# Retention, then a truncated-quadratic MoE layer, then a SoLU layer: blocks of 512 tokens, weight conversion kept off GpSimd, activation as a maximum read from PSUM, decay tables in the attention, state decay on ScalarE

## The chip, the cores and the metric

The kernel runs on one core of one Trainium2 chip. A core has TensorE (PE in the profile, its weight loads PEld), VectorE (DVE), ScalarE (ACT), GpSimd (POOL) and SyncE (SP), which here issues every DMA. The metric is the device time of one execution in microseconds; a version is judged by the median of its runs.

## The reference

Three layers follow each other, all in float32.

```python
# attention: B, H, S, D = 4, 8, 768, 64; gamma = 1 - 2**(-5 - head)
for t in range(S):
    state = gamma * state + k[t] (outer) v[t]
    y[t] = q[t] @ state / sqrt(D)
x = y as [3072 tokens, 512]
# first layer: 512 -> 2048 -> 512
h = x @ w_in
g = h where h >= 1, 0 where h <= -1, else (h + 1)**2 / 4
x2 = g @ w_out
# second layer: 512 -> 1024 -> 512
u = h2 * softmax(h2), h2 = x2 @ w2_in
out = (layer norm of u, times g_ln) @ w2_out
```

The weights arrive as float64.

## The kernel before

**Phase A** is attention and the first layer. The 3072 tokens go in blocks of BLK = 384 (eight blocks), and d_ff = 2048 in 16 parts f of 128. A *slot* is one block with one part f. `moe_h` (line 319) makes h of the slot with 12 matmuls (L325): each float32 operand is held as a sum of two float32r parts, and the three products high-high, low-high, high-low are added in PSUM over four parts of d_model. The activation follows (L337 to L342), its result is again split in two (L121 on ScalarE, L122 on VectorE), and `moe_out` (line 347), two slots later, adds 12 more matmuls (L360) into four PSUM banks `acc`. At the end of a block the four banks are copied out (L368 to L373) and stored to DRAM. 128 slots in all. Their order is not block by block at first: block 0 with f 0 to 5, block 1 with f 0 to 11, block 0 with f 6 to 15, block 1 with f 12 to 15, then whole blocks (L275). So new weights are taken up slowly; an unfinished block's sum is parked in DRAM (`x2p`).

**Weights** are loaded by L130 and converted by `conv_w` (L133): ScalarE takes the high word's absolute value (L139) and the low word (L142), VectorE clips, shifts and merges the sign (L140, L143, L144), GpSimd adds the two as integers (L145), ScalarE rounds to the high part (L149), and the low part is a subtraction (L150), on GpSimd for 34 of the 48 conversions and on VectorE for 14. Phase A needs 32 conversions, one pair per part f; the 16 conversions of the second layer run in the last block (L417 to L419), two per slot, those of w2_out with one more VectorE step (L147).

**Attention** goes in 24 units of 128 tokens with all heads, `attention` (L157), each a generator whose steps are taken in given slots (L283 to L290). The first six units (NF32) work in plain float32, the others split queries and keys in float32r parts (L197 to L200, L206 to L210). A unit scales v by a decay column (L183), masks the scores (L211 or L215), multiplies scores by v (L233) and the state by the queries (L229), scales the result by a table (L238), splits it (L121, L122), and renews the state (L245 to L254).

**Phase B** is the second layer, 24 tiles of 128 tokens, lines 432 to 537: 24 matmuls L464, softmax and norm on VectorE and ScalarE, 8 transposes L505, 24 matmuls L516.

**Order.** Every engine runs its own list in order. The lists are made by a scheduler that takes the order of issue in the program as priority; attention units from the seventh on and the loads of the first eight parts f are raised by 1000. PSUM has four banks `acc` (shared with the attention of block 0 and phase B), two banks for h (`ps_h`) and two for attention (`ps_a`).

Of the kernel before, what the change touches and what calls it, by code (L numbers as in the profile page):

```python
# [26 lines left out]
BLK = 384  # L27
# [6 lines left out]
# words of the high half of a float64, read as float32: 2^-127 and the largest float32r  # L34
LO_I = (0,1)
LO_O = range(4,16)
LO_2 = 0
V_POOL = 3
DMA_ORDER = -99
PSV = 0  # L40
HPW = 0
HPL = 8
SA = 6
SB = 12
LD = 6
CL = 3
HPC = 0
PHB = 3
XL_POOL = 0
QL_POOL = 0  # L50
NF32 = 6
WM_BUFS = 3
WP_BUFS = 3
QK_BUFS = 3
QS_BUFS = 1
KV_BUFS = 1
QN_BUFS = 1
GATE = 6
SM_BUFS = 3
# [14 lines left out]
def kernel(  # L74
# [23 lines left out]
    wp = ctx.enter_context(tc.tile_pool(name="wp", bufs=33))  # L98
# [8 lines left out]
    neg1 = const.tile([128, 1], F32, tag="neg1", name="neg1")  # L107
    mask = const.tile([128, 1, C], F32, tag="mask", name="mask")
# [8 lines left out]
    def split(src, hi, lo, hi_eng=None, lo_eng=None):  # L117
        if hi_eng is ve:
            ve.tensor_copy(hi, src)
        else:  # L120
            sc.activation(hi, src, AF.Copy)  # L121
        (lo_eng or ve).tensor_tensor(out=lo, in0=src, in1=fl(hi), op=ALU.subtract)  # L122

# [9 lines left out]
    def conv_w(raw, scale=None, lo_eng=None):  # L133
        lw, hw = raw[:, :, 0], raw[:, :, 1]
        m = cv.tile([128, 512], F32, tag="wm", name="wm", bufs=WM_BUFS)
        p = cv.tile([128, 512], F32, tag="wp", name="wp", bufs=WP_BUFS)
# [14 lines left out]
        return w[:, 0, :], w[:, 1, :]  # L151

# [1 line left out]
    # Heads go in pairs (even, odd); the even one takes partitions 0-63 of queries, keys and  # L154
    # state, the odd one 64-127, and TensorE works on both halves of its array at a time.
    # In x the halves of pairs 2 and 3 are swapped, and so are the rows of w_in.
    def attention(u, env):  # L157
# [26 lines left out]
        sm = []  # L184
        if exact:
            yield
            qp = [ppool.tile([128, NPAIR, C], F32, tag=ptag, name=f"qp{o}") for o in range(2)]
            for p in range(NPAIR):
                for o in range(2):
                    r = slice(64 * o, 64 * o + 64)  # L190
                    pe.matmul(qp[o][:, p, :], qk[r, 1, p, :], qk[r, 0, p, :], start=True, stop=True)
        for o in range(2):
            if not exact:
                raw = qks[o]
                kh = cv.tile([128, NPAIR, C], F32R, tag="wm", name="kh", bufs=WM_BUFS)
                qs = attp.tile([128, NPAIR, 2, C], F32R, tag="qs", name="qs", bufs=QS_BUFS)
# [186 lines left out]
    for s in range(min(min(sched), -LD - 1), 0):  # L383
# [5 lines left out]
        if s == DMA_ORDER:  # L389
            order.close()  # L390
# [207 lines left out]
```

## Time and profile before

| what | value |
|---|---|
| median of 3 runs | 972.96 us (972.27 to 973.82) |
| profiled execution, its span | 969.7 us |
| TensorE busy | 936.3 us, 97% |
| weight loads busy | 856.5 us, 88% |
| VectorE busy | 741.9 us, 77% |
| ScalarE busy | 455.6 us, 47% |
| GpSimd busy | 201.0 us, 21% |
| instructions | 14961 |

The profile is of one execution. It gives the span from the first to the last instruction; the time of an execution also has what lies around the span, and the median is 3.3 us above it. Times of single matmuls overlap, since the next one enters the array before the last has left: the distance between starts is what one costs.

### The profile page before, as it was taken

Reading aid. Unit: us, or ns where it says so; the run is one execution under the profiler, and the core shown is the slowest. Engines: PE = TensorE matmul, PEld = TensorE weight load, DVE = VectorE, ACT = ScalarE, POOL = GpSimd, SP = SyncE. Lnnn points to the kernel's source line nnn. Section 1 sums busy time; section 2 is a strip of 40 time slices with the busy share of each in tenths; the row PEclk is TensorE's granted clock in tenths of the full one; section 3 lists DMA queues with packets and bytes.
Section 4 is the critical chain, followed back from the end, with each engine's and each line's share of the span. In section 5 each row is a group of like instructions: output and inputs, shape, how many; then the busy total and the mean of one; then the engine's idle time right before and its main releaser. Section 6 shows DMA issues by size and latency. Waiting matters only on the chain.

```text
span 969.7 us, 14961 instructions
## 1 busy us (share of the span) xinstructions
PE 936.3 (97%) x5560; PEld 856.5 (88%) x5560; DVE 741.9 (77%) x1593; ACT 455.6 (47%) x905; POOL 201.0 (21%) x177
## 2 busy tenths in 40 slices
PE   8798898999999999999999999989999999999998
PEld 7588888999999999999999999969888888888886
DVE  6999999877666666655664574997788888888885
ACT  3557676545545545544553464664433333333322
POOL 2754544212211221111220120662000000000000
PEclk9899999999999999999999999999999999999999
DMA  9902823154233232420320230311111011010000
GB/s 366 360 1 82 250 82 114 48 169 126 79 98 116 92 97 80 128 77 22 114 72 12 107 143 1 122 64 69 66 55 42 35 55 54 23 61 28 22 23 33
DMA packets 31465, 87.03 MB, mean 90 GB/s; under 512 B 4384, under 2 KB 10656, under 8 KB 31392
## 3 DMA queue, kind: packets, MB, share of 16 engines
q1 hardware_dynamic: 31392, 86.08, 26.9%
q8 instruction: 44, 0.72, 0.3%
q14 instruction: 29, 0.24, 0.1%
HBM read 71.90 MB, written 14.16 MB: 89 GB/s over the span
## 4 chain that ended last, share of the span: by engine, by line
PE 74%; DVE 18%; issue 3%; ACT 2%; DMA 2%; SPq 0%; POOL 0%; ACTq 0%; DVEq 0%; POOLq 0%
PE acc L360 19%; PE hp L325 19%; PE h2p L464 14%; PE op L516 14%; DVE wm L144 3%; DVE cs L340 3%; DVE wm L140 2%; PE pv L233 2%; PE tp L505 2%; DVE gl L122 2%; PE qp L206 2%; DVE wm L143 2%; DVE cs L337 2%; PE pv L229 2%; DVE w L150 1%
## 5 line engine op out<-in xcount | busy, mean ns | idle before, releaser
L360 PE MATMUL acc<-gh,w 128*128 128x384 f32 x1024 | 214.3, 339 | 9.6 <-ACT gh L121 7.6
L325 PE MATMUL hp<-xh,w 128*128 128x384 f32 x1024 | 209.6, 340 | 5.6 <-ACT rr L338 3.9
L360 PEld LDWEIGHTS acc<-gh,w 128*128 128x128 f32 x1024 | 180.1, 189 | 15.4 <-ACT gh L121 10.4
L325 PEld LDWEIGHTS hp<-xh,w 128*128 128x128 f32 x1024 | 179.0, 189 | 12.2 <-ACT rr L338 6.2
L338 ACT ACTIVATE rr<-hp,neg 128x384 f32<-128x384 f32 x128 | 74.1, 579 | 161.4 <-DVE cs L337 161.2
L340 DVE TENSOR_TENSOR cs<-cs,rr 128x384 f32<-128x384 f32 x128 | 86.0, 672 | 77.7 <-ACT cs L339 76.8
L360 PE MATMUL acc<-gl,w 128*128 128x384 f32 x512 | 121.7, 338 | 4.8 <-DVE gl L122 4.8
L325 PE MATMUL hp<-xl,w 128*128 128x384 f32 x512 | 111.8, 338 | 0.0
L122 DVE TENSOR_TENSOR gl<-cs,gh 128x384 fp32r<-128x384 f32 x128 | 85.5, 668 | 26.7 <-ACT gh L121 24.5
L121 ACT ACTIVATE gh<-cs 128x384 fp32r<-128x384 f32 x128 | 66.8, 522 | 65.7 <-DVE cs L340 65.5
L464 PE MATMUL h2p<-w,x2h 128*128 128x512 f32 x384 | 97.4, 395 | 0.0
L360 PEld LDWEIGHTS acc<-gl,w 128*128 128x128 f32 x512 | 90.3, 188 | 8.1 <-DVE gl L122 7.5
L337 DVE TENSOR_SCALAR cs<-hp 128x384 f32<-128x384 f32 x128 | 70.5, 551 | 32.3 <-PE hp L325 31.8
L325 PEld LDWEIGHTS hp<-xl,w 128*128 128x128 f32 x512 | 91.7, 190 | 0.5 <-DVE xl L122 0.3
L516 PE MATMUL op<-w,lh 128*128 128x512 f32 x384 | 91.4, 390 | 0.2 <-ACT lh L121 0.2
L145 POOL TENSOR_TENSOR wm<-wm,wp 128x512 int32<-128x512 int32 x48 | 69.1, 1440 | 88.0 <-DVE wm L144 70.6
L516 PEld LDWEIGHTS op<-w,lh 128*128 128x128 f32 x384 | 71.9, 188 | 15.4 <-ACT lh L121 0.5
L464 PEld LDWEIGHTS h2p<-w,x2h 128*128 128x128 f32 x384 | 70.5, 188 | 13.5
L339 ACT ACTIVATE cs<-cs,half 128x384 f32<-128x384 f32 x128 | 77.6, 606 | 2.5 <-DVE cs L337 2.5
L150 POOL TENSOR_TENSOR w<-wm,w 128x512 fp32r<-128x512 f32 x34 | 49.6, 1461 | 52.2 <-ACT w L149 51.9
L211 POOL TENSOR_SCALAR_AFFINE_SELECT sm<-sm 128x512 f32<-128x512 f32 x36 | 36.3, 1010 | 99.6 <-DVE sm L210 99.6
L254 POOL TENSOR_TENSOR state<-state,gdec 64x256 f32<-64x256 f32 x32 | 22.0, 688 | 165.1 <-DVE state L253 163.9
(79 smaller groups left out, 1299.7 us busy)
## 6 DMA issues: line engine op xcount, KB each, us to landing
qk<-in_qk_t_dram SPq DMA_DIRECT2D x72, 256.0 KB, 3.8
kv<-in_kv_t_dram SPq DMA_DIRECT2D x24, 512.0 KB, 3.8
w_raw<-in_w_in_dram SPq DMA_DIRECT2D x24, 512.0 KB, 7.3
w_raw<-in_w_out_dram SPq DMA_DIRECT2D x24, 512.0 KB, 6.7
x2d<-xs SPq DMA_DIRECT2D x32, 192.0 KB, 2.0
x2r<-x2d SPq DMA_DIRECT2D x8, 768.0 KB, 4.3
out_dram<-o SPq DMA_DIRECT2D x24, 256.0 KB, 2.0
qn<-in_qk_t_dram SPq DMA_DIRECT2D x15, 256.0 KB, 3.1
```

What stands on the lines that cost most here:

```text
L121: sc.activation(hi, src, AF.Copy)
L122: (lo_eng or ve).tensor_tensor(out=lo, in0=src, in1=fl(hi), op=ALU.subtract)
L145: gp.tensor_tensor(out=mi, in0=mi, in1=p.bitcast(I32), op=ALU.add)
L150: (lo_eng or gp).tensor_tensor(out=w[:, 1, :], in0=m, in1=fl(w[:, 0, :]), op=ALU.subtract)
L325: pe.matmul(hp, l[:, k * 128:(k + 1) * 128], r[:, k, :], start=(n == 0), stop=(n == 3 * KD - 1))
L337: ve.tensor_scalar(cs, hp, -1.0, 1.0, op0=ALU.max, op1=ALU.min)
L338: sc.activation(rr, hp, AF.Relu, bias=neg1)
L339: sc.activation(cs, cs, AF.Square, bias=half, scale=0.5)
L340: ve.tensor_tensor(out=cs, in0=cs, in1=rr, op=ALU.add)
L360: pe.matmul(acc[d][:, :BLK], l[:, d * 128:(d + 1) * 128], r, start=(first and m == 1), stop=(last and m == 3))
L464: pe.matmul(hps[n], l[:, k, :], w2i[k, n][part], start=(m == 0), stop=(m == 3 * KD - 1))
L516: pe.matmul(op, l[:, f, :], w2o[f][part], start=(n == 0), stop=(n == 3 * NF2 - 1))
```

## The change

- BLK is 512: six blocks, 96 slots, each with 24 matmuls of 512 columns in place of 384. NF32 becomes 8 (two blocks of four units). The attention's places in the slots follow the new block (PER = 4), and weights are converted four slots ahead instead of three, loaded seven ahead instead of six.
- `conv_w` has no GpSimd step: the integer add and the low part go to VectorE; the scale of w2_out goes into the rounding on ScalarE and into the low part's instruction. The second layer's conversions go at 2, 1, 2, 1, ... per slot from f = 2 to 12.
- The activation is max(h, ((clip(h) + 1)/2)^2): ScalarE's relu (L338) is gone, and VectorE's last step reads h from PSUM.
- The mask and both decays of the scores become one table `dmat` by which VectorE multiplies the scores; the scaling of v, the scaling of the result (L238) and the masking on GpSimd (L211) go. Instead the queries for the state are multiplied by `qdec` (VectorE for the first eight units, GpSimd after), and the keys for the state by the decay column on GpSimd, except in the last unit of a sequence. `tables` makes the two tables at the start.
- The state is decayed by four ScalarE instructions before the sum, not on GpSimd after it. The state's matmuls are issued before the result is split.
- Fewer buffers: sm and qk have 2 instead of 3; xs shares three buffers with cs. The raised priority of the first weight loads goes.

```diff
-BLK = 384
+BLK = 512
...
-LD = 6
-CL = 3
+LD, CL = 7, 4
+NF32 = 2 * CPB
+GATE = 2 * CPB
+PER = 4
...
-        gp.tensor_tensor(out=mi, in0=mi, in1=p.bitcast(I32), op=ALU.add)
-        if scale is not None:
-            ve.tensor_scalar(m, m, scale, None, op0=ALU.mult)
+        ve.tensor_tensor(out=mi, in0=mi, in1=p.bitcast(I32), op=ALU.add)
         w = wp.tile([128, 2, 512], F32R, tag="w", name="w")
-        sc.activation(w[:, 0, :], m, AF.Copy)
-        (lo_eng or gp).tensor_tensor(out=w[:, 1, :], in0=m, in1=fl(w[:, 0, :]), op=ALU.subtract)
+        hi, lo = w[:, 0, :], w[:, 1, :]
+        if scale is None:
+            sc.activation(hi, m, AF.Copy)
+            ve.tensor_tensor(out=lo, in0=m, in1=fl(hi), op=ALU.subtract)
+        else:
+            sc.activation(hi, m, AF.Copy, scale=scale)
+            ve.scalar_tensor_tensor(lo, m, scale, fl(hi), op0=ALU.mult, op1=ALU.subtract)
...
-        (gp if u >= V_POOL else ve).tensor_tensor(out=kv[:, 1], in0=kv[:, 1], in1=vdec.to_broadcast([128, H, D]), op=ALU.mult)
...
+            if not first:
+                qn = attp.tile([128, NPAIR, C], F32, tag="qn", name="qn", bufs=1)
+                ve.tensor_tensor(out=qn, in0=qk[:, 0], in1=qdec, op=ALU.mult)
+        elif not first:
+            gp.tensor_tensor(out=qn, in0=qn, in1=qdec, op=ALU.mult)
+        if not last:
+            gp.tensor_tensor(out=kv[:, 0], in0=kv[:, 0], in1=vdec.to_broadcast([128, H, D]), op=ALU.mult)
...
-                gp.affine_select(out=t, in_=t, pattern=[[0, NPAIR], [1, C]], compare_op=ALU.is_ge,
-                                 fill=0.0, base=0, channel_multiplier=-1)
+                ve.tensor_tensor(out=t, in0=t, in1=dmat[:, o], op=ALU.mult)
...
-        for g in range(2):
-            d = slice(2 * g, 2 * g + 2)
-            ve.tensor_tensor(out=xt[:, d], in0=pv[g], in1=xtab[:, d], op=ALU.mult)
-        split(xt, xh[:, :, tk], xl[:, :, tk], lo_eng=gp if XL_POOL else None)
+        split(pv, xh[:, :, tk], xl[:, :, tk])
...
+        if not first:
+            for p in range(NPAIR):
+                sc.activation(st[:, p, :], st[:, p, :], AF.Copy, scale=gdec[:, p, :])
...
-                ve.tensor_tensor(out=d, in0=sp[r], in1=d, op=ALU.add)
-                gp.tensor_tensor(out=d, in0=d, in1=g, op=ALU.mult)
+                ve.tensor_tensor(out=st[r, :, r], in0=sp[r], in1=st[r, :, r], op=ALU.add)
...
+    def tables():
+        nc.sync.dma_start(vdec, vdec_d)
+        for o in range(2):
+            for dup in range(2):
+                nc.sync.dma_start(dmat[64 * dup:64 * dup + 64, o], xtab_d[64 * o:64 * o + 64])
+        nc.sync.dma_start(gdec, gdec_d)
+        nc.sync.dma_start(qdec, xtab_d)
+        for o in range(2):
+            ve.tensor_tensor(out=dmat[:, o], in0=dmat[:, o], in1=vdec[:, o::2].to_broadcast([128, NPAIR, C]), op=ALU.mult)
+            gp.affine_select(out=dmat[:, o], in_=dmat[:, o], pattern=[[0, NPAIR], [1, C]], compare_op=ALU.is_ge,
+                             fill=0.0, base=0, channel_multiplier=-1)
+        gp.tensor_tensor(out=qdec, in0=qdec, in1=gdec.to_broadcast([128, NPAIR, C]), op=ALU.mult)
...
-        x = (k - 3, SA - 3 + k, X2 + 3 * k)[blk] if blk < 3 else base[blk] - NF + PER * k + SHIFT
+        x = (k - CPB, SA - CPB + k)[blk] if blk < 2 else base[blk] - NF + PER * k + 2
...
-            sc.activation(rr, hp, AF.Relu, bias=neg1)
-            sc.activation(cs, cs, AF.Square, bias=half, scale=0.5)
-        ve.tensor_tensor(out=cs, in0=cs, in1=rr, op=ALU.add)
+        sc.activation(cs, cs, AF.Square, bias=half, scale=0.5)
+        ve.tensor_tensor(out=cs, in0=hp, in1=cs, op=ALU.max)
...
-            if f >= 2:
-                w2_conv(2)
-                w2_step(2)
+            if 2 <= f < 13:
+                w2_conv(2 - f % 2)
+                w2_step(2 - f % 2)
```

## Rows read from the trace of the kernel before

**Rows 1.** Stretches: length; busy us of PE, PEld, DVE, ACT, POOL; clock; DMA share; GB/s.
```profile
5.60:71.30 65.70, 56.28 (x433) 47.02 (x432) 62.82 (x95) 31.54 (x55) 37.70 (x31) 0.92 0.63 250
71.30:155.00 83.70, 73.48 (x413) 68.32 (x414) 80.01 (x122) 59.48 (x113) 36.85 (x27) 0.98 0.42 131
...
200.00:600.00 400.00, 399.50 (x2650) 388.12 (x2649) 254.58 (x466) 197.41 (x402) 70.99 (x74) 1.00 0.30 92
600.00:686.00 86.00, 79.36 (x430) 73.89 (x430) 70.04 (x100) 49.81 (x92) 39.22 (x27) 1.00 0.21 73
686.00:969.70 283.70, 279.72 (x1329) 233.00 (x1327) 234.38 (x742) 88.99 (x191) 0.00 (x0) 1.00 0.12 42
```

**Rows 2.** Chain of waits that ended last, by line, of the first 160 us alone.
```profile
by line: issue 11.7%; DVE wm L144 10.2%; DVE wm L140 9.3%; DVE cs L340 8.4%; DVE wm L143 7.6%; DVE gl L122 7.0%; DVE cs L337 5.5%; DVE w L150 5.2%; DMA kv<-in_kv_t_dram 3.5%; DVE xl L122 2.7%; PE acc L360 2.2%; DVE sm L215 2.2%; DMA w_raw<-
```

**Rows 3.** Timeline of PE: start us, length us, line, shape, count.
```profile
401.86 1.55 PE L360 MATMUL acc<-gh,w 128*128 128x384 f32 x8
403.24 0.85 PE L360 MATMUL acc<-gl,w 128*128 128x384 f32 x4
...
404.28 0.64 PE L206 MATMUL qp<-qs,kh 128*128 128x256 f32 x4
404.76 1.21 PE L325 MATMUL hp<-xh,w 128*128 128x384 f32 x6
...
818.02 3.79 PE L516 MATMUL op<-w,lh 128*128 128x512 f32 x16
821.64 1.98 PE L516 MATMUL op<-w,ll 128*128 128x512 f32 x8
```

**Rows 4.** Lines of PE from 200 to 600 us, by form: count, busy us, mean ns.
```profile
L360 PE MATMUL acc<-gh,w 128*128 128x384 f32 x654 | 134.7, 335 | 0.5 <-DVE xs L373 0.5
...
L325 PE MATMUL hp<-xl,w 128*128 128x384 f32 x324 | 69.9, 334 | 0.0
...
L233 PE MATMUL pv<-sm,kv 128*64 128x128 f32 x256 | 20.5, 280 | 0.0
```

**Rows 5.** Lines of VectorE and GpSimd, first 155 us, by form: count, busy us, mean ns.
```profile
L144 DVE SCALAR_TENSOR_TENSOR wm<-w_raw,wm 128x512 uint32<-128x512 uint32 x28 | 24.3, 869 | 0.1
...
L150 DVE TENSOR_TENSOR w<-wm,w 128x512 fp32r<-128x512 f32 x11 | 12.7, 1151 | 0.0
...
L145 POOL TENSOR_TENSOR wm<-wm,wp 128x512 int32<-128x512 int32 x28 | 39.4, 1409 | 51.3 <-DVE wm L144 37.1 <-ACT cs L339 8.3 <-ACT wp L142 2.0
```

**Rows 6.** Single lines over the whole span: count, min/median/max ns, first and last start.
```profile
L140 DVE TENSOR_SCALAR wm<-wm x48: 410/420/1522, 15.4 to 657.1; 128x512 f32<-128x512 f32 x48
...
L144 DVE SCALAR_TENSOR_TENSOR wm<-w_raw,wm x48: 672/681/1776, 17.4 to 659.8; 128x512 uint32<-128x512 uint32 x48
...
L337 DVE TENSOR_SCALAR cs<-hp x128: 542/550/560, 31.2 to 678.5; 128x384 f32<-128x384 f32 x128
...
L340 DVE TENSOR_TENSOR cs<-cs,rr x128: 544/558/1651, 36.5 to 680.3; 128x384 f32<-128x384 f32 x128
...
L183 POOL TENSOR_TENSOR kv<-kv,vdec x21: 1042/1045/1494, 24.4 to 537.8; 128x512 f32<-128x512 f32 x21
```

**Rows 7.** Timeline around 103 us: VectorE, then GpSimd.
```profile
103.56 0.42 DVE L143 TENSOR_SCALAR wm<-wm 128x512 uint32<-128x512 uint32 x1
103.89 1.78 DVE L150 TENSOR_TENSOR w<-wm,w 128x512 fp32r<-128x512 f32 x1
105.59 0.54 DVE L337 TENSOR_SCALAR cs<-hp 128x384 f32<-128x384 f32 x1
106.06 0.68 DVE L144 SCALAR_TENSOR_TENSOR wm<-w_raw,wm 128x512 uint32<-128x512 uint32 x1
106.66 0.41 DVE L140 TENSOR_SCALAR wm<-wm 128x512 f32<-128x512 f32 x1
...
103.72 1.40 POOL L145 TENSOR_TENSOR wm<-wm,wp 128x512 int32<-128x512 int32 x1 [2.70 <-DVE wm L144]
```

**Rows 8.** The page's costliest groups: one line of ScalarE, count, busy us, mean ns.
```profile
L338 ACT ACTIVATE rr<-hp,neg 128x384 f32<-128x384 f32 x128 | 74.1, 579 | 161.4 <-DVE cs L337 161.2
```

More of the change, by code (lines that the diff above doesn't have):

```diff
@@ L115, in fl, with split @@
         return t.bitcast(F32)
[L117 to L122, printed above, removed]
+    def split(src, hi, lo):
+        sc.activation(hi, src, AF.Copy)
+        ve.tensor_tensor(out=lo, in0=src, in1=fl(hi), op=ALU.subtract)
     wi, wo = {}, {}
@@ L163, in attention @@
         exact = u < NF32
-        kv = (wp if exact else attp).tile([128, 2, H, D], F32, tag="w" if exact else "kv", name="kv", bufs=None if exact else KV_BUFS)
+        kv = (wp if exact else attp).tile([128, 2, H, D], F32, tag="w" if exact else "kv", name="kv",
+                                          bufs=None if exact else 1)
+        qn = None
         with (ExitStack() if u < GATE else tc.issue_after(state["last_w"].ins)):
@@ L224, in attention @@
         tk = slice(cb * C, cb * C + C)
-        pv = [ppool.tile([128, 2, C], F32, tag=ptag, name=f"pv{g}") for g in range(2)]
+        pv = ppool.tile([128, NPAIR, C], F32, tag=ptag, name="pv")
         if not first:
             for p in range(NPAIR):
-                pe.matmul(pv[p // 2][:, p % 2, :], st[:, p, :], qn[:, p, :],
-                          start=(p % 2 == 0), stop=False, skip_group_check=True)
+                pe.matmul(pv[:, p, :], st[:, p, :], qn[:, p, :],
+                          start=(p == 0), stop=False, skip_group_check=True)
@@ L231, in attention @@
         for p in range(NPAIR):
             for o in range(2):
-                pe.matmul(pv[p // 2][64 * o:64 * o + 64, p % 2, :], kv[:, 1, 2 * p + o, :], sm[o][:, p, :],
-                          start=(first and p % 2 == 0), stop=(p % 2 == 1), skip_group_check=True)
-        xt = attp.tile([128, NPAIR, C], F32, tag="xt", name="xt", bufs=1)
-        for g in range(2):
-            d = slice(2 * g, 2 * g + 2)
-            ve.tensor_tensor(out=xt[:, d], in0=pv[g], in1=xtab[:, d], op=ALU.mult)
@@ L239, in attention @@
-        split(xt, xh[:, :, tk], xl[:, :, tk], lo_eng=gp if XL_POOL else None)
+                pe.matmul(pv[64 * o:64 * o + 64, p, :], kv[:, 1, 2 * p + o, :], sm[o][:, p, :],
+                          start=(first and p == 0), stop=(p == NPAIR - 1), skip_group_check=True)
+        if not last:
+            sp = ppool.tile([128, NPAIR, D], F32, tag=ptag, name="sp")
+            for p in range(NPAIR):
+                for o in range(2):
+                    pe.matmul(sp[64 * o:64 * o + 64, p, :], kv[:, 0, 2 * p + o, :], kv[:, 1, 2 * p + o, :],
+                              start=True, stop=True)
@@ L240, in attention @@
+        split(pv, xh[:, :, tk], xl[:, :, tk])
         if last:
             return
-        sp = ppool.tile([128, NPAIR, D], F32, tag=ptag, name="sp")
-        for p in range(NPAIR):
-            for o in range(2):
-                pe.matmul(sp[64 * o:64 * o + 64, p, :], kv[:, 0, 2 * p + o, :], kv[:, 1, 2 * p + o, :],
-                          start=True, stop=True)
+        if not first:
+            for p in range(NPAIR):
+                sc.activation(st[:, p, :], st[:, p, :], AF.Copy, scale=gdec[:, p, :])
@@ L296, in att_slot @@
                 gens[u] = attention(u, env)
-            with (tc.high_priority(offset=HP_ATT) if HP_ATT and u >= HP_FROM else ExitStack()):
+            with (tc.high_priority(offset=HP_ATT) if u >= NF32 else ExitStack()):
                 next(gens[u], None)
@@ L385 @@
         if s == min(sched):
-            for t, d in ((vdec, vdec_d), (gdec, gdec_d), (xtab, xtab_d)):
-                nc.sync.dma_start(t, d)
+            tables()
         weights_slot(s)
-        if s == DMA_ORDER:
-            order.close()
     w2 = [(w2_in[k, n], (k, n), w2i, None) for k in range(KD) for n in range(2)] + \
@@ L401, in w2_conv @@
         for raw, key, dst, scale in [w2raw.pop(0) for _ in range(min(n, len(w2raw)))]:
-            dst[key] = conv_w(raw, scale, lo_eng=ve if LO_2 else None)
+            dst[key] = conv_w(raw, scale)
     pend = []
```

109 lines of the change are left out of this document (29 added, 80 removed).

## The prediction

> **What bounds the kernel now.** I read the stretches first [rows 1], because the share of busy time over the whole span mixes phases with different limits. Three phases show. From 200 to 600 us TensorE is busy 399.5 of 400 us and VectorE 254.6: TensorE bounds. From 686 us on, phase B, TensorE is busy 279.7 of 283.7: TensorE again, and the change touches nothing there but the size of a load. Up to 155 us VectorE is busy 62.8 of 65.7 and then 80.0 of 83.7 us, while TensorE has gaps and a mean clock of 0.92: VectorE bounds. From 600 to 686 us VectorE has 70.0 of 86.0 and TensorE is idle for 6.6. The chain of the first 160 us confirms it [rows 2]: its lines are VectorE's conversion (L144, L140, L143, L150) and activation (L340, L122, L337); TensorE's first line has 2.2%.
>
> What does a matmul cost? Starts tell it, not lengths [rows 3]: eight of 384 columns from 401.86 to 403.24, so about 173 ns; four of 256 in 0.48 us, 120 ns; sixteen of 512 from 818.02 to 821.64, 226 ns. All three are (columns + 32) / 2.4 GHz: 173.3, 120.0, 226.7. Weight loads do not bound at 384, since at 256 the same 128x128 load goes through in 120 ns.
>
> The 200 to 600 us stretch holds 1950 first-layer matmuls (four rows, the first and last shown) and 256 of L233, 16 per unit, so 16 units [rows 4]: 400 - 0.5 - 1950 x 0.1733 = 61.5 us, 3.85 us of TensorE per attention unit.
>
> **What TensorE loses now.** By 71.3 us, where the seventh slot starts, it has done six h and four output halves (120 matmuls, 20.8 us) and six units (23.1), 43.9 of the 65.7 us since 5.6: 21.8 lost. From there to 686 remain 2952 matmuls (511.7), 18 units (69.3) and the 15 phase B instructions of 1344 that are missing after 686 [rows 1] (3.4): 584.4 of 614.7, 30.3 lost, nearly none of it in 200 to 600.
>
> **What stretches VectorE.** L140 has a median of 420 ns and a maximum of 1522, L144 681 and 1776, L340 558 and 1651; L337, which reads PSUM, stays at 542 to 560 [rows 6]. The timeline shows who does it [rows 7]: GpSimd starts L145 at 103.72 for 1.40 us, VectorE's L150 starts at 103.89 and takes 1.78 instead of about 0.68. In the first 155 us the means are 869 for L144 and 1151 for L150 [rows 5]. So work that GpSimd does beside VectorE is largely paid for on VectorE.
>
> **The change, part by part.** VectorE's prices are distances of starts where nothing stretches [rows 7]: 0.33 us for L143 and L140's kind, 0.47 for 384 columns, 0.60 for 512 with two inputs.
>
> *Conversion.* 0.33 + 0.33 + 0.60, and two new instructions. The low part is L150, 0.60 unstretched. An int32 add on VectorE is in no row: between 0.60, which its uint32 neighbour L144 takes, and the 1.41 us that GpSimd's L145 takes [rows 5]; I take 0.60, the row of the same engine and word size. Together 2.46 us. The scale of w2_out costs nothing new: it rides on instructions that are there, and L147 goes. ScalarE keeps three steps.
>
> *Blocks.* 3072 matmuls x 0.1733 = 532.5 us become 2304 x 0.2267 = 522.2: 10.3 us saved wherever TensorE bounds. [...]
>
> *Activation.* Per 512-token slot VectorE has three instructions of 0.60, 1.8 us; ScalarE loses L338. The maximum holds the bank of h until VectorE has read it a second time: 0.60, ScalarE's square, 0.60, some 2.2 us in all. The bank is wanted again two slots later, 2 x 5.44 - 2.72 = 8.2 us after its last matmul. So nothing, unless VectorE's queue is over 6 us long; behind a blocked matmul stand that slot's output matmuls and attention.
>
> *Attention.* TensorE's work stays at 24 units. An exact unit costs VectorE two table products, the query product, the split and two halves of the state (0.34 each): about 3.0. A split unit: 6.3 (four splits of 0.60 to 0.65, four sums of 256 columns at 0.34, two table products, the split of the result, two halves of the state). In 200 to 600 us VectorE has 145 us to spare, which hides them. ScalarE's four decay steps of 128 columns a unit are in no row: between nothing (ScalarE is idle half of that stretch) and 0.58 each, what L338 takes for three times the columns [rows 8], 2.3 us in the chain of a unit at the start. I take nothing, as VectorE has other units' and conversions' steps meanwhile. They wait for the same matmuls as the split queued ahead of them, so nothing new stands behind them. GpSimd's scaling of keys (1.05 us [rows 6]) is waited for by the state's matmuls, with the next slot's behind them; it is issued a slot or more ahead, and uncovered would cost 1 us a unit. GpSimd falls to some 20 key and 13 query products, about 38 us.
>
> *Tables and loads.* Four more transfers on SP's queue and 0.5 MB ahead of the second unit, and block 0 wants four units before its first matmul: I charge 3 us, between 0 and 6. The weights' loss of priority is covered by the fourth unit's work on VectorE. Buffers of sm, qk and xs: nothing while VectorE has time to spare, up to 2 us per block end otherwise. The remaining GpSimd products can each stretch one VectorE step by 1.1 us, up to 8 at the start; I charge 1.
>
> **The sum.** VectorE up to the seventh slot: 8 units (23.5), tables 1.2, 12 conversions (29.5), six slots (10.8): 65. From 5.6, with the 2.9 us of idleness it has there now and the 4 charged, the seventh slot starts at 77. Then slots 6 to 17: VectorE 12 x 1.8 + 12 x 2.46 + 6.3 = 57, TensorE 12 x 5.44 + 3.85 = 69. Slots 18 to 27: VectorE 53, TensorE 64. The bound passes to TensorE. In the last block, f 2 to 12, VectorE has 16 x 2.46 + 11 x 1.8 = 59 against TensorE's 60: even, so some waiting stays. I put TensorE's losses after 77 us at 15 (6 up to slot 27, 1 in the middle, 8 in the last block), where now they are 30.
>
> So 77 + 2184 x 0.2267 (495.0) + 16 units (61.6) + 3.4 + 15 = 652 for the end of phase A, and 283.7 for phase B: a span of 936, against 969.7. The runs' median lies 3.3 us above the profiled span; with that, 939 us.
>
> **The rivals.**
> *Losses stay (962.7).* The starting phase may be held by latency, four engines handing a tile round with in-order queues, and not by VectorE's sum; then its 52 us of losses stay and only the 10.3 us of columns are won. For it: TensorE waits there for short chains, and the scheduler places everything anew. Against it: VectorE is busy 96% of that time. 0.18.
> *Conversion on VectorE is dear (slower, about 985).* If the stretch does not go, or the int32 add costs more, and a conversion takes 1.6 us more (the two new steps at L150's stretched 1.15, the others at their means), then 12 conversions before the seventh slot cost 19, the next 20 exceed TensorE by 10, and the last 16 cost 25, of which 8 are charged already: 939 + 46. The point where it eats the whole gain of 34 is near 1.2 us more, 3.6 us a conversion. Against it: [rows 7] show the stretch beside a GpSimd instruction, and GpSimd has almost nothing left. 0.07.
> *The h bank is held (953).* If VectorE's queue makes the maximum late in the 28 slots with conversions, half a microsecond each. 0.10.
> *Columns alone set a matmul's price (947).* [...] Three sizes in [rows 3] speak against it. 0.03.
> The forecast has 0.62.
>
> **The numbers.** 0.2% of 973, about 2 us, is what a measurement of this kernel can tell from no change. All cases but the dear conversion are faster; I leave 0.03 for no difference: 0.90 faster, 0.03 same, 0.07 slower. The range goes down to 922, where the start and the last block lose almost nothing (15 less), and up to 965, which takes in the rivals at 947, 953 and 962.7 and an int32 add at GpSimd's price (0.8 us more a conversion: 10 before the seventh slot, 4 to 12 in the last block, so 953 to 961); outside it are the slow case and some of the forecast's lower tail.
>
> **What the profile after would show.** First-layer matmuls of 512 columns 226.7 ns apart; L140's and L144's counterparts with means near 0.42 and 0.69; GpSimd near 40 us and VectorE near 670 instead of 742; the seventh slot's h near 77 us; phase A's end near 652. The forecast is wrong if the conversion's steps stay stretched, if the int32 add takes over 1 us, or if TensorE's idle time between 77 and 240 us exceeds 15.

## The result, and the profile after

The changed kernel takes 931.39 us (median of 4 runs, 930.84 to 932.33) against 972.62 us for the kernel before, measured beside it (971.59 to 973.82): a ratio of 0.9567, 95% interval 0.9545 to 0.959. The forecast was 939 us, range 922 to 965.

Lines of the changed kernel that are met below, with those of before: L108, L111, L112 are the conversion's steps on VectorE (L140, L143, L144), L113 the integer add (L145), L117 and L118 high and low part (L149, L150); L306 makes h (L325), L312 clips it (L337), L314 is the maximum (L340), L90 the low half of a split (L122), L334 the output half of a slot (L360), L347 adds a parked sum, L180 is ScalarE's part of the split of the keys, L223 the state's decay.

The stretches, columns as in [rows 1], over the whole of the changed kernel:

```profile
5.60:75.00 69.40, 62.16 (x524) 50.27 (x524) 63.82 (x116) 36.43 (x71) 11.97 (x10) 0.98 0.72 281
75.00:155.00 80.00, 78.08 (x368) 64.52 (x369) 78.27 (x140) 55.19 (x96) 5.88 (x4) 0.98 0.42 132
155.00:240.00 85.00, 85.00 (x437) 70.29 (x436) 59.30 (x102) 38.29 (x72) 4.12 (x3) 1.00 0.29 81
240.00:560.00 320.00, 314.66 (x1737) 261.33 (x1737) 203.23 (x339) 135.11 (x262) 25.64 (x20) 1.00 0.33 96
560.00:645.00 85.00, 85.00 (x376) 70.38 (x375) 60.94 (x107) 40.30 (x66) 0.00 (x0) 1.00 0.23 80
645.00:929.30 284.30, 280.20 (x1331) 233.38 (x1329) 234.34 (x742) 89.23 (x191) 0.00 (x0) 1.00 0.11 40
```

From 75 to 155 us TensorE is now busy 78.1 of 80, though VectorE is as full as before; the last stretch of phase A has no idle TensorE time, and phase B, from 645, is as long as it was (284.3 against 283.7). The engines' totals and the chain by engine, from the page, and below them the chain by engine of before:

```profile
PE 909.6 (98%) x4808; PEld 754.5 (81%) x4808; DVE 700.1 (75%) x1542; ACT 395.8 (43%) x757; POOL 48.3 (5%) x42
PE 91%; DVE 5%; DMA 2%; issue 1%; ACT 0%; SPq 0%; POOL 0%; ACTq 0%; DVEq 0%; POOLq 0%
```
```profile
PE 74%; DVE 18%; issue 3%; ACT 2%; DMA 2%; SPq 0%; POOL 0%; ACTq 0%; DVEq 0%; POOLq 0%
```

VectorE's share of the chain that ended last is 5%, where it was 18%. The conversion's lines over the whole span (count, min/median/max ns), then in the first 155 us (count, busy us, mean ns), where [rows 5] had 869 for L144 and 1151 for L150:

```profile
L108 DVE TENSOR_SCALAR wm<-wm x48: 416/423/856, 22.1 to 598.0; 128x512 f32<-128x512 f32 x48
L112 DVE SCALAR_TENSOR_TENSOR wm<-w_raw,wm x48: 679/687/699, 23.0 to 602.5; 128x512 uint32<-128x512 uint32 x48
```
```profile
L118 DVE TENSOR_TENSOR w<-wm,w 128x512 fp32r<-128x512 f32 x27 | 18.9, 708 | 0.1
L113 DVE CUSTOM_DVE_ANT_0 wm<-wm,wp 128x1024 uint16<-128x1024 uint16 x27 | 18.5, 688 | 0.1
```

L144's maximum of 1776 ns [rows 6] has become 699. The integer add stands in the trace as CUSTOM_DVE_ANT_0 over 1024 halfwords, with a mean of 0.688 us, where L118's is 0.708 and L112's median 0.687; on the timeline (start us, length us) the next step starts 0.60 us behind it:

```profile
109.87 0.69 DVE L113 CUSTOM_DVE_ANT_0 wm<-wm,wp 128x1024 uint16<-128x1024 uint16 x1
110.47 0.43 DVE L108 TENSOR_SCALAR wm<-wm 128x512 f32<-128x512 f32 x1
```

**Where the time came from.** The sum in the prediction can be done on any run: the time, less 5.6, less the first-layer matmuls so far by their price, less the units by 3.85, is what TensorE has lost by then (rough by a microsecond or two, as units in hand are counted by their finished part). In the column of 700 us phase B's 512-column matmuls are taken off as well, its transposes are not, which leaves up to 2 us too much there. In us:

| lost by | 80 | 155 | 240 | 300 | 560 | 700 us | runs' median |
|---|---|---|---|---|---|---|---|
| before | 21.8 | 37.3 | 41.6 | 41.9 | 40.8 | 53.0 | 972.62 |
| after | 16.4 | 18.2 | 19.1 | 24.0 | 21.6 | 25.6 | 931.39 |
| e2_before_conv_on_vectore | 21.8 | 23.7 | 25.7 | 25.2 | 23.8 | 27.1 | 945.74 |
| e1_conv_on_gpsimd | 21.6 | 39.3 | 41.3 | 49.9 | 46.1 | 53.5 | 960.34 |
| e5_gpsimd_reads | 36.7 | 67.7 | 68.0 | 69.1 | 68.4 | 68.5 | 986.27 |
| e3_after_384 | 25.3 | 28.9 | 30.0 | 34.6 | 45.0 | 47.5 | 965.70 |
| e11_384_three_qk | 23.2 | 27.8 | 28.1 | 27.0 | 23.6 | 27.1 | 943.65 |
| e7_attention_of_before | 15.9 | 20.5 | 20.7 | 33.3 | 35.2 | 38.5 | 944.93 |
| e12_three_qk | 16.4 | 24.5 | 25.0 | 36.7 | 32.7 | 37.8 | 944.51 |

At the end of phase A the same sum needs no such care. After has lost some 22 us at 645 us (639.4 - 522.2 - 92.4 for the 24 units, less 2.9 for 13 matmuls of phase B that come earlier); before had lost 21.8 + 30.3 = 52.1 at 686 us. So of the 40.4 us by which the span fell, 10.3 are columns and 30 are losses that went.

### The profile page after: what moved, and what is told of

It is laid out like the page before. It is cut to its first block, busy times and chain, and to the rows that moved or that the text cites. A ratio compares the mean times of both kernels' runs of the same rounds, so it can differ in the third digit from the quotient of the medians.

```text
span 929.3 us, 12929 instructions
## 1 busy us (share of the span) xinstructions
PE 909.6 (98%) x4808; PEld 754.5 (81%) x4808; DVE 700.1 (75%) x1542; ACT 395.8 (43%) x757; POOL 48.3 (5%) x42
## 4 chain that ended last, share of the span: by engine, by line
PE 91%; DVE 5%; DMA 2%; issue 1%; ACT 0%; SPq 0%; POOL 0%; ACTq 0%; DVEq 0%; POOLq 0%
PE acc L334 27%; PE hp L306 27%; PE h2p L433 14%; PE op L485 14%; PE tp L474 2%; PE pv L210 2%; PE pv L206 2%; PE qp L188 1%; DMA qk<-in_qk_t_dram 1%; PE sp L216 1%; PE qp L163 1%; DVE wm L112 1%; DVE wm L113 1%; DMA xs<-x2p 1%; DMA vdec<-in_vdec_dram 0%
## 5 line engine op out<-in xcount | busy, mean ns | idle before, releaser
L306 PE MATMUL hp<-xh,w 128*128 128x512 f32 x768 | 200.1, 395 | 7.2 <-DVE cs L314 2.9
L334 PE MATMUL acc<-gh,w 128*128 128x512 f32 x768 | 198.4, 391 | 1.6 <-DVE xs L347 1.6
L306 PEld LDWEIGHTS hp<-xh,w 128*128 128x128 f32 x768 | 141.9, 189 | 38.5 <-DVE cs L314 3.7
L334 PEld LDWEIGHTS acc<-gh,w 128*128 128x128 f32 x768 | 143.1, 188 | 32.3 <-DVE xs L347 2.3
L313 ACT ACTIVATE cs<-cs,half 128x512 f32<-128x512 f32 x96 | 69.3, 723 | 138.9 <-DVE cs L312 138.5
L334 PE MATMUL acc<-gl,w 128*128 128x512 f32 x384 | 110.7, 391 | 0.0
L306 PE MATMUL hp<-xl,w 128*128 128x512 f32 x384 | 105.7, 392 | 0.1
L312 DVE TENSOR_SCALAR cs<-hp 128x512 f32<-128x512 f32 x96 | 65.8, 688 | 39.1 <-PE hp L306 36.0
L90 DVE TENSOR_TENSOR gl<-cs,gh 128x512 fp32r<-128x512 f32 x96 | 68.4, 713 | 33.0 <-ACT gh L89 32.5
L314 DVE TENSOR_TENSOR cs<-hp,cs 128x512 f32<-128x512 f32 x96 | 66.1, 690 | 35.3 <-ACT cs L313 35.1
L89 ACT ACTIVATE gh<-cs 128x512 fp32r<-128x512 f32 x96 | 60.4, 629 | 58.4 <-DVE cs L314 58.2
L306 PEld LDWEIGHTS hp<-xl,w 128*128 128x128 f32 x384 | 72.0, 189 | 15.6 <-DVE xl L90 0.5
L334 PEld LDWEIGHTS acc<-gl,w 128*128 128x128 f32 x384 | 71.6, 188 | 15.1
L433 PE MATMUL h2p<-w,x2l 128*128 128x512 f32 x192 | 51.6, 390 | 0.0
```

The costliest lines, as they stand in the source:

```text
L90: ve.tensor_tensor(out=lo, in0=src, in1=fl(hi), op=ALU.subtract)
L306: pe.matmul(hp, l[:, k * 128:(k + 1) * 128], r[:, k, :], start=(n == 0), stop=(n == 3 * KD - 1))
L312: ve.tensor_scalar(cs, hp, -1.0, 1.0, op0=ALU.max, op1=ALU.min)
L313: sc.activation(cs, cs, AF.Square, bias=half, scale=0.5)
L314: ve.tensor_tensor(out=cs, in0=hp, in1=cs, op=ALU.max)
L334: pe.matmul(acc[d][:, :BLK], l[:, d * 128:(d + 1) * 128], r, start=(first and m == 1), stop=(last and m == 3))
```

## The experiments

### What the conversion's move is worth

**e2_before_conv_on_vectore**: the kernel before, with the two GpSimd steps of the conversion alone moved.

```diff
-        gp.tensor_tensor(out=mi, in0=mi, in1=p.bitcast(I32), op=ALU.add)
+        ve.tensor_tensor(out=mi, in0=mi, in1=p.bitcast(I32), op=ALU.add)
...
-        (lo_eng or gp).tensor_tensor(out=w[:, 1, :], in0=m, in1=fl(w[:, 0, :]), op=ALU.subtract)
+        ve.tensor_tensor(out=w[:, 1, :], in0=m, in1=fl(w[:, 0, :]), op=ALU.subtract)
```

> The kernel before with all of the conversion's GpSimd work on VectorE, nothing else. Theory: the stretch goes (L140 near 0.42, L144 near 0.69 in the mean), a slot's VectorE work in the start falls from about 2.0 to 1.5 us, TensorE's losses there fall by 15 to 25 us: 948 to 958 us. Rival, the start is held by hand-overs between engines or by the size of the blocks: 966 or more. Rival, VectorE gets dearer: above 973.

Measured 945.74 us, ratio 0.9721 (0.9706 to 0.9736): 27 us from this edit alone, a little more than expected. By the table half of it is won by 155 us and some 10 after 560, where the second layer's weights are converted. **e1_conv_on_gpsimd** is the other way round, the changed kernel with the add and the unscaled low part on GpSimd again.

```diff
-        ve.tensor_tensor(out=mi, in0=mi, in1=p.bitcast(I32), op=ALU.add)
+        gp.tensor_tensor(out=mi, in0=mi, in1=p.bitcast(I32), op=ALU.add)
...
-            ve.tensor_tensor(out=lo, in0=m, in1=fl(hi), op=ALU.subtract)
+            gp.tensor_tensor(out=lo, in0=m, in1=fl(hi), op=ALU.subtract)
```

> The kernel after with the conversion's integer add and unscaled low part back on GpSimd (88 instructions). Theory, VectorE pays for what GpSimd does beside it: GpSimd back at about 170 us, means of the shift and sign steps back from 0.45 and 0.69 to about 0.65 and 0.85, so a conversion costs VectorE about as much as it saves; with 512-token blocks there is slack behind it, so 5 to 10 us are lost at the start and in the last block: 936 to 942 us. Rival A, the conversion's move is where most of the 41 us came from: 955 or more. Rival B, it is free once the blocks are large: within 2 us of 931.

Measured 960.34 us, 0.9872 (0.9855 to 0.9888): 29 us given back. The expectation missed; its rival A came, the conversion's move is where most of the gain was. The stretch from 75 to 155 us in e2, then in e1:

```profile
75.00:155.00 80.00, 78.42 (x469) 76.30 (x468) 76.63 (x155) 61.55 (x120) 5.70 (x5) 1.00 0.47 147
```
```profile
75.00:155.00 80.00, 68.84 (x367) 56.05 (x364) 71.09 (x99) 48.69 (x89) 48.10 (x35) 0.91 0.42 126
```

In e2 VectorE carries up to two more steps a conversion and TensorE still fills up; in e1 TensorE loses 11 us here. Of e1, in three views: VectorE's lines in the first 155 us (count, busy us, mean ns | idle before), TensorE's first wait (total us, times, longest), and the timeline behind its longest (start us, length us):

```profile
L112 DVE SCALAR_TENSOR_TENSOR wm<-w_raw,wm 128x512 uint32<-128x512 uint32 x26 | 25.8, 994 | 0.4
L111 DVE TENSOR_SCALAR wm<-wm 128x512 uint32<-128x512 uint32 x26 | 23.7, 910 | 0.5
...
L314 DVE TENSOR_TENSOR cs<-hp,cs 128x512 f32<-128x512 f32 x14 | 9.4, 684 | 0.4 <-ACT cs L313 0.4
```
```profile
PE hp L306 <- DVE cs L314: 15.7, 5, 5.7
```
```profile
103.69 3.78 PE L306 MATMUL hp<-xh,w 128*128 128x512 f32 x8 [5.67 <-DVE cs L314]
```

The stretch is back (994 against 687), and L314, which reads h from PSUM, is untouched at 684. VectorE's queue now runs so late that the maximum holds the bank of h: the prediction's third rival, in a kernel where GpSimd works. The eight matmuls behind that gap last 3.78 us, 449 ns from start to start (103.69 to 107.28), where eight last 1.98 at a granted clock of 1.00 (after, 108.94 to 110.75), 226 ns apart: the clock granted from 103.69 to 107.3 us is 0.50 of full speed, so this gap cost more than its length.

**Contention or waiting?** e1 and e2 change both: in before ScalarE also waits 18 us for GpSimd's results (11.0 + 4.2 + 2.8). **e5_gpsimd_reads** is e2 with two GpSimd additions beside each of phase A's 32 conversions; they read a table that is there already (`env0["d"]` is `xtab`), and nothing waits for them:

```diff
+        dq = cv.tile([128, NPAIR, C], F32, tag="dq", name="dq", bufs=1)
+        for _ in range(2 if state.get("att", True) else 0):
+            gp.tensor_tensor(out=dq, in0=env0["d"], in1=env0["d"], op=ALU.add)
```

> The kernel before with the conversion on VectorE, and beside each of the 32 first-layer conversions two GpSimd additions of 128x512 (reading a constant table, written to a scratch tile that nothing reads), so GpSimd is as busy as before but nobody waits for it. Theory, VectorE pays for GpSimd's work by contention: VectorE's conversion and two-input steps in the first 155 us are stretched as before (means of L140 0.6, L144 0.85 us) and the time lies 10 to 20 us over the same kernel without the additions. Rival, before lost by waiting for GpSimd's results: within 3 us of that kernel.

Measured 986.27 us, 1.0128 (1.0112 to 1.0144): 40.5 us more than e2 (39.6 by the ratios to before), over twice what was expected, and slower than the kernel before. The longest wait of an engine for GpSimd in it is 0.2 us. **e6_gpsimd_writes** has memsets in their place, about as long in all (83.4 us of GpSimd in the first 155, against 79.9) but reading nothing.

```diff
+        dq = cv.tile([128, 860], F32, tag="dq", name="dq", bufs=1)
+        for _ in range(3 if state.get("att", True) else 0):
+            gp.memset(dq, 1.0)
```

> As the run with GpSimd additions, but three GpSimd memsets of 860 elements a conversion instead, which read nothing. [...]

Measured 964.27 us, 0.9889 (0.9863 to 0.9914): 18.5 us more than e2 (16.3 by the ratios), under half of e5's loss. VectorE's lines in the first 155 us (count, busy us, mean ns | idle before), e2 with the lines of before, then e5, whose lines lie one further (L144 shifts, L145 merges the sign, L146 adds, L345 is the activation's sum, L342 its clip), then e6 (L143, L144, L145, L343, L340):

```profile
L144 DVE SCALAR_TENSOR_TENSOR wm<-w_raw,wm 128x512 uint32<-128x512 uint32 x29 | 20.4, 702 | 0.1
L145 DVE CUSTOM_DVE_ANT_0 wm<-wm,wp 128x1024 uint16<-128x1024 uint16 x29 | 19.8, 682 | 0.0
L143 DVE TENSOR_SCALAR wm<-wm 128x512 uint32<-128x512 uint32 x29 | 13.1, 451 | 0.0
L340 DVE TENSOR_TENSOR cs<-cs,rr 128x384 f32<-128x384 f32 x23 | 12.6, 550 | 0.0
```
```profile
L145 DVE SCALAR_TENSOR_TENSOR wm<-w_raw,wm 128x512 uint32<-128x512 uint32 x23 | 24.6, 1074 | 0.1
L146 DVE CUSTOM_DVE_ANT_0 wm<-wm,wp 128x1024 uint16<-128x1024 uint16 x22 | 22.8, 1035 | 0.0
L144 DVE TENSOR_SCALAR wm<-wm 128x512 uint32<-128x512 uint32 x23 | 16.2, 706 | 0.0
L345 DVE TENSOR_TENSOR cs<-cs,rr 128x384 f32<-128x384 f32 x14 | 10.7, 762 | 0.0
L342 DVE TENSOR_SCALAR cs<-hp 128x384 f32<-128x384 f32 x14 | 7.5, 544 | 0.0
```
```profile
L144 DVE SCALAR_TENSOR_TENSOR wm<-w_raw,wm 128x512 uint32<-128x512 uint32 x27 | 20.4, 758 | 0.0
L145 DVE CUSTOM_DVE_ANT_0 wm<-wm,wp 128x1024 uint16<-128x1024 uint16 x27 | 18.3, 676 | 0.0
L143 DVE TENSOR_SCALAR wm<-wm 128x512 uint32<-128x512 uint32 x27 | 17.9, 663 | 0.0
L343 DVE TENSOR_TENSOR cs<-cs,rr 128x384 f32<-128x384 f32 x21 | 11.4, 543 | 0.0
L340 DVE TENSOR_SCALAR cs<-hp 128x384 f32<-128x384 f32 x22 | 11.9, 544 | 5.9 <-PE hp L328 5.9
```

Beside the additions, steps with two SBUF inputs stretch (1074, 1035 and 762, where e2 has 702, 682 and 550) and the one-input step too (706 for 451); beside the memsets the one-input step stretches (663), the merge of the sign a little (758 for 702), and the two-input sums don't (676, 543); the clip, which reads PSUM, stays at 544 in both. What couples the two engines, and why memsets leave the sums alone, no run shows. So GpSimd work beside a full VectorE costs by contention, by which no more is meant than that VectorE's steps last longer without any wait for a result: 40.5 us for 64 additions in the first 155 us. VectorE's own steps account for it: their count in e5 times the excess of their mean over e2's, line by line in those 155 us, is an estimated 42 us. In e6 the same sum is some 8 us; where the rest of its 18.5 comes from stays open. How e2's 27 us divide between the stretch and ScalarE's 18 us of waits was not isolated either.

### What the blocks are worth

**e3_after_384**: the changed kernel with the old block.

```diff
-BLK = 512
+BLK = 384
...
-PER = 4
+PER = 5
```

> The kernel after with blocks of 384 tokens (NF32 and the places of the attention follow, PER = 5). Theory: 10.3 us of TensorE columns come back, and a converted weight has 31% less TensorE work to hide under, which loses 3 to 10 us more in the start and the last block: 945 to 952 us. Rival, the blocks give the columns and nothing else: 940 to 943. Rival, the blocks are nearly the whole gain: 960 or more.

Measured 965.70 us, 0.9935 (0.9918 to 0.9952): far over the expectation, and slower than e2, which has the same blocks and the old attention. The second rival's number came, but not by its cause. ScalarE's waits (total us, times, longest) show what e2 hardly has (1.9 us in 5):

```profile
ACT kh L180 <- DMA qk<-in_qk_t_dram: 72.7, 29, 4.8
```

The split of the keys, in order on ScalarE, waits for the transfer of the queries and keys, whose tile has two buffers where before it had three. **e11_384_three_qk** gives e3 the third:

```diff
-                    qk = attp.tile([128, 2, NPAIR, C], F32, tag="qk", name="qk", bufs=2)
+                    qk = attp.tile([128, 2, NPAIR, C], F32, tag="qk", name="qk", bufs=3)
```

> The kernel after at 384 tokens (965.7 us) with three buffers for queries and keys instead of two. Theory: with two, the next unit's load starts only when this unit's half is split, ScalarE waits 72.7 us for it in 29 places and TensorE loses 15 us between 240 and 560; with three these come back: 949 to 955 us, still above the 945.7 of before with the conversion moved, since the start stays worse by 5. Rival, the loss is that the state's sum holds one of attention's two PSUM banks: 963 or more.

Measured 943.65 us, 0.9707 (0.9692 to 0.9722): better than expected. The buffer was worth 22 us at 384, and the wait has fallen to 2.2 us. Against after it is the nearest pair of sizes: 943.65 - 931.39 = 12.3 us, 10.3 of which are columns, at 173.3 ns for 384 and 226.7 for 512. The other 2 are what blocks save besides, or more, if the 5 us that after, with its two qk buffers, loses from 240 to 300 and e11 does not are those buffers' (see the part on the attention).

### The activation alone

**e4_before_max**: the kernel before with the maximum in place of sum and relu.

```diff
-            sc.activation(rr, hp, AF.Relu, bias=neg1)
...
-        ve.tensor_tensor(out=cs, in0=cs, in1=rr, op=ALU.add)
+        ve.tensor_tensor(out=cs, in0=hp, in1=cs, op=ALU.max)
```

> The kernel before with the activation as a maximum read from PSUM, nothing else; ScalarE's relu goes. Theory: the maximum has one operand in PSUM and is not stretched, L340's mean of 0.83 us in the first 155 us falls to 0.55, 20 slots save 5 us of VectorE there: 964 to 970 us. Rival, the bank of h is held until the second reading and TensorE waits for it: 973 to 985.

Measured 972.38 us, 0.9983 (0.9966 to 1.0): nothing that can be told, where 964 to 970 was expected. 74.1 us of ScalarE work [rows 8] went, and no time with it. Theory and rival both came about: in the first 155 us the maximum's mean is 546 ns where the sum's was 825, but TensorE now waits for it while the bank of h is held (total us, times, longest):

```profile
PE hp L325 <- DVE cs L337: 16.7, 11, 3.4
```

In before the like wait, for the relu, is 3.9 us. The conversion's clip also stretches more (777 ns for 633); what each of these is worth was not isolated.

### The attention, its places and its buffers

**e7_attention_of_before**: the changed kernel with the attention of before (mask on GpSimd, v and result scaled, state decayed on GpSimd, the state's matmuls behind the split), two buffers each of sm and qk as in the change.

```diff
-                ve.tensor_tensor(out=t, in0=t, in1=dmat[:, o], op=ALU.mult)
+                gp.affine_select(out=t, in_=t, pattern=[[0, NPAIR], [1, C]], compare_op=ALU.is_ge,
+                                 fill=0.0, base=0, channel_multiplier=-1)
...
-        split(pv, xh[:, :, tk], xl[:, :, tk])
+        for g in range(2):
+            d = slice(2 * g, 2 * g + 2)
+            ve.tensor_tensor(out=xt[:, d], in0=pv[g], in1=xtab[:, d], op=ALU.mult)
+        split(xt, xh[:, :, tk], xl[:, :, tk])
...
-            for p in range(NPAIR):
-                sc.activation(st[:, p, :], st[:, p, :], AF.Copy, scale=gdec[:, p, :])
+                gp.tensor_tensor(out=d, in0=d, in1=g, op=ALU.mult)
```

> The kernel after with the attention of before (v scaled, mask on GpSimd, result scaled by a table, state decayed on GpSimd), all else as after. Theory: attention's VectorE work is hidden under TensorE after the start, and in the start GpSimd's steps stretch VectorE by some 5 us, while the tables' late start (first score product at 9.2 us against 6.9) is won back: 929 to 936 us. Rival, the decay tables and the state's decay on ScalarE carry a share of the gain: 940 or more.

Measured 944.93 us, 0.9716 (0.9702 to 0.973): 13.5 us over after, missed. The table shows the main place: 12.6 lost from 240 to 300 us, where block 1 ends and block 2 begins, against 4.9 in after. TensorE's timeline there and the stretch from 240 to 260 us, both of e7 (L304 makes h, L312 is the maximum, L95 the high half of a split), then both of after:

```profile
253.72 5.81 PE L304 MATMUL hp<-xh,w 128*128 128x512 f32 x16 [1.38 <-ACT xh L95]
264.23 3.51 PE L304 MATMUL hp<-xh,w 128*128 128x512 f32 x8 [2.41 <-DVE cs L312]
```
```profile
240.00:260.00 20.00, 15.44 (x67) 12.04 (x66) 8.94 (x17) 4.98 (x11) 5.21 (x7) 0.74 0.52 145
```
```profile
254.21 2.14 PE L306 MATMUL hp<-xh,w 128*128 128x512 f32 x8 [1.42 <-DVE cs L314]
265.92 0.73 PE L334 MATMUL acc<-gh,w 128*128 128x512 f32 x2 [1.58 <-DVE xs L347]
```
```profile
240.00:260.00 20.00, 16.87 (x113) 13.12 (x112) 14.20 (x26) 8.05 (x17) 3.19 (x2) 1.00 0.54 146
```

VectorE is busy only 8.94 of 20 us in e7: no engine is full; h waits for a unit's split result (xh), and the clock falls to a mean of 0.74 of full speed with it. ScalarE's timeline shows why that result is late (L177 splits keys):

```profile
249.19 0.63 ACT L177 ACTIVATE kh<-qk 128x512 fp32r<-128x512 f32 x1 [2.65 <-DMA qk<-in_qk_t_dram]
252.51 0.63 ACT L177 ACTIVATE kh<-qk 128x512 fp32r<-128x512 f32 x1 [2.70 <-DMA qk<-in_qk_t_dram]
253.05 0.61 ACT L95 ACTIVATE xh<-xt 128x512 fp32r<-128x512 f32 x1
```

The unit's result (xt) is written by 251.3 us, but the split that h needs stands in ScalarE's queue behind a split of keys that waits for its transfer, as in e3. So TensorE's 1.38 us at 253.72 are the ring of two qk buffers, reached through ScalarE; in all e7 has 72.0 us of such waits. This is read from the trace: no run gives e7 the third buffer, and the other gaps of e7 were not traced back. **e9_units_earlier** (after, with the units from the ninth on two slots earlier) and **e10_attention_of_before_earlier** (e7 with the same edit) ask whether the place in the order decides.

```diff
-        x = (k - CPB, SA - CPB + k)[blk] if blk < 2 else base[blk] - NF + PER * k + 2
+        x = (k - CPB, SA - CPB + k)[blk] if blk < 2 else base[blk] - NF + PER * k
```

> The kernel after with the attention units from the ninth on placed two slots earlier, no other change. The profile after has a wait that before had not: ScalarE's split of keys waits for the queries' and keys' transfer 25 times, 44.5 us, 4.2 at most, and behind it in ScalarE's queue stand the splits of x and the squares; TensorE loses 5 us of it at the start of block 2. Theory: two slots more give that place its slack back, the start has some VectorE work moved into it: 925 to 930 us. Rival, the earlier units cost the start what they give later: 930 to 935.

> The kernel after with the attention of before (944.9 us), and the units from the ninth on two slots earlier. Theory: the 13.5 us that the old attention costs there are the place at the start of block 2 (12.6 us lost between 240 and 300), a matter of when units are due and not of their work: 930 to 937 us. Rival, the old attention costs by its work on VectorE and GpSimd: 942 or more.

Measured 933.68 us (0.9602, 0.9587 to 0.9617) and 946.34 us (0.9732, 0.9708 to 0.9757): no gain in either, both expectations missed. The old attention keeps its cost of 13 us with the earlier places too.

**e8_buffers** gives the pool that cs and xs share four buffers instead of three (gl gets two, to make room).

```diff
-        cs = moe.tile([128, BLK], F32, tag="cs", name="cs", bufs=3)
+        cs = moe.tile([128, BLK], F32, tag="cs", name="cs", bufs=4)
...
-        gl = moe.tile([128, BLK], F32R, tag="gl", name="gl", bufs=GB)
+        gl = moe.tile([128, BLK], F32R, tag="gl", name="gl", bufs=2)
...
-                xs = moe.tile([128, BLK], F32, tag="cs", name="xs", bufs=3)
+                xs = moe.tile([128, BLK], F32, tag="cs", name="xs", bufs=4)
```

> The kernel after with four instead of three buffers shared by cs and xs, paid for by two instead of three of gl. Theory: the 5.3 us that TensorE loses between 240 and 280 us, where block 1 ends and its parked sum is read back into that pool, fall to 2 or less, and the low part of g is written after the output matmuls that need its buffer: 927 to 930 us. Rival, gl's missing buffer makes each slot wait: above 933.

Measured 931.89 us, 0.9569 (0.9555 to 0.9583): no change, and by the table's sum e8 still loses 7.5 us from 240 to 300; so the 5 us that after loses there are not that pool's, unless gl's missing buffer costs as much. **e12_three_qk** asks whether they are the queries' transfer, for which ScalarE waits in after as in e3:

```profile
ACT kh L180 <- DMA qk<-in_qk_t_dram: 44.5, 25, 4.2
```

It gives qk the third buffer and takes the room from gl (two) and from the shared pool (two).

```diff
-                    qk = attp.tile([128, 2, NPAIR, C], F32, tag="qk", name="qk", bufs=2)
+                    qk = attp.tile([128, 2, NPAIR, C], F32, tag="qk", name="qk", bufs=3)
...
-        cs = moe.tile([128, BLK], F32, tag="cs", name="cs", bufs=3)
+        cs = moe.tile([128, BLK], F32, tag="cs", name="cs", bufs=2)
...
-        gl = moe.tile([128, BLK], F32R, tag="gl", name="gl", bufs=GB)
+        gl = moe.tile([128, BLK], F32R, tag="gl", name="gl", bufs=2)
...
-                xs = moe.tile([128, BLK], F32, tag="cs", name="xs", bufs=3)
+                xs = moe.tile([128, BLK], F32, tag="cs", name="xs", bufs=2)
```

> The kernel after with three buffers for queries and keys, paid for by two instead of three of gl and of the pool that cs and xs share. Theory: ScalarE's waits for that transfer fall from 44 to under 15 us; TensorE can win back at most the 5 us at the start of block 2, and the smaller shared pool may cost 1 to 2 us at each of the seven block ends: 925 to 936 us. It tells whether those waits cost TensorE anything at 512 tokens.

Measured 944.51 us, 0.9721 (0.9695 to 0.9748): 13 us slower and outside the expectation, though ScalarE's waits for that transfer fall to 9 us, as expected. A line of TensorE's timeline near 108 us, then one of VectorE's where block 1 ends:

```profile
108.38 3.53 PE L306 MATMUL hp<-xh,w 128*128 128x512 f32 x8 [3.85 <-DVE cs L314]
...
240.03 0.69 DVE L312 TENSOR_SCALAR cs<-hp 128x512 f32<-128x512 f32 x1 [3.61 <-DMA x2d<-xs]
```

With two buffers the clip of a new slot waits for the store of a finished block, 3.61 us here (6.2 us in five such waits, 2.5 in two in after); the wait of TensorE for the maximum, 3.85 us, is longer than any such wait in after, whose three sum to 2.9. So the smaller rings (the pool or gl) cover whatever the third qk buffer gives, and whether the qk wait is after's 5 us stays open. The total of that wait doesn't tell a cost: e8 has 71.0 us of it in 25 waits, and after's time. What counts is what stands behind a wait.

## Why the prediction was right, and where its terms were off

*The bound and what stretches VectorE.* Right. e2 takes 27 us away by moving two steps onto the engine that was full, and e5 puts more than all of them back. "Losses stay" falls with e2: the starting phase was held by VectorE's stretched sum. "Conversion is dear" did not happen: the add's starts are 0.60 us apart, the low end of its bounds.

*Blocks.* Right. The prediction's formula for a matmul is worked out from the three pitches of [rows 3], where 128 columns more cost 53 ns. No run shows the saving that the rival "columns alone" has in its 947 us; e11 and after lie 12.3 us apart, and the rival is ruled out by the pitch that after's timeline shows, twelve matmuls of 512 columns from 108.94 to 111.66, 226.7 ns each:

```profile
108.94 1.98 PE L306 MATMUL hp<-xh,w 128*128 128x512 f32 x8
110.75 1.07 PE L306 MATMUL hp<-xl,w 128*128 128x512 f32 x4
111.66 0.62 PE L334 MATMUL acc<-gh,w 128*128 128x512 f32 x2
```

*Activation at nothing, the h bank held at nothing.* Right in after: TensorE waits 2.9 us in all for L314. The 15.7 us in e1 and the 16.7 in e4 show the condition that the step named, a late VectorE queue.

*Attention at nothing.* Right at 384 with three qk buffers: e2 and e11, old and new attention, differ by 2 us (with the activation and the places). Wrong as a general step: at 512 with two qk buffers the old attention costs 13.5 us. The prediction asked whether VectorE has time to spare; it had (8.94 us busy of 20), and TensorE waited all the same, for the end of a unit's chain, one link of which is ScalarE's wait for the qk transfer. The old attention at 512 with three qk buffers was not tried.

*ScalarE's decay.* Taken as nothing, bound 0.58 each; it lasts 0.386, and the only waits for it in the trace are 1.0 us of VectorE and 0.2 of ScalarE:

```profile
L223 ACT ACTIVATE state<-state,gdec x64: 384/386/403, 14.5 to 477.8; 128x128 f32<-128x128 f32 x64
```

*Buffers of sm, qk and xs: "nothing while VectorE has time to spare".* This step failed in kind: VectorE had time, and the wait was ScalarE's, for a transfer that could not start. Of its size at 512 with the new attention the runs give only a bound, after's 5 us between 240 and 300; at 384 it is 22 us. From 240 to 560 us, where the forecast charged 1 us, after lost 2.5 and e7 14.5 (table). So it is the new attention that keeps the smaller rings cheap at 512, which neither of these two steps foresaw: here the number owes something to luck.

*The losses.* Forecast were 13.4 by the seventh slot, 6 to slot 27, 1 in the middle and 8 in the last block, 28.4 in all; after shows 16.4 by 80 us, about 3 to 240, about 5 to 300 and none from there, some 22. That is nearly all of the 6.7 us by which the span (929.3) lies under the 936 forecast. By 76.1 us five slots had their h, not six; the 24 matmuls of the sixth and the seventh then come together, the first twelve behind a 2.12 us wait, 345 ns apart at a mean granted clock of 0.66 from 76.11 to 80.5. So the seventh's began between 77 and 79 us, where 77 was forecast:

```profile
76.11 4.35 PE L306 MATMUL hp<-xh,w 128*128 128x512 f32 x12 [2.12 <-ACT w L117]
```

The last block's 8 us were the worst-sized term. VectorE and TensorE were counted even there, and some waiting charged for it. VectorE was indeed full while the second layer was converted, 29.87 of 30 us from 570 to 600, but TensorE waited nowhere from 560 to 645; the last conversion was through by 609 us, and phase A ended at 645 instead of 652. The conversions' results are wanted in phase B alone; that this is why no slot waited is argued, not shown. VectorE's 700 us (670 forecast) and GpSimd's 48 (near 40) were low guesses without consequence.

No run beats the changed kernel; e8 equals it.

## What to carry to other kernels

Work given to GpSimd beside a VectorE that set the pace was paid for in VectorE's own steps here (40.5 us for e5's 64 additions), so count GpSimd's steps against the engine that they may stretch before calling them free, and test it with dummy GpSimd work that nobody waits for. When a larger tile takes room from another ring of buffers, ask which in-order queue waits for the transfer that the ring no longer holds ahead, and what stands behind that wait: at 384 tokens here a third buffer was worth 22 us, more than the 12 by which blocks of 512 came out ahead.

## What was not expected of the hardware

GpSimd's additions cost more than their number suggested: 40.5 us for 64 of 1.25 us each in the first 155 us, 0.63 us of the kernel's time apiece, while memsets cost 18.5 us for 96, 0.19 apiece. The estimated 42 us of stretch on VectorE cover e5's loss, and VectorE is busy 79.93 of the 80 us from 75 to 155. TensorE's clock falls beside it, to a mean of 0.83 of full speed where e2 has 1.00; whether that costs anything of its own is not shown.

```profile
75.00:155.00 80.00, 55.27 (x280) 51.97 (x280) 79.93 (x111) 43.38 (x79) 43.44 (x35) 0.83 0.29 94
```
